# A linear-attention and feed-forward kernel on one core: one-pass softplus, exponentials gathered in two places of a tile, float32r earlier in the first tile

## The chip, the cores and the metric

The kernel runs on one core of one Trainium2 chip. A core has five engines that run side by side, each through its own queue in order: TensorE (PE, with weight loads counted apart as PEld) multiplies matrices, VectorE (DVE) and ScalarE (ACT) work element by element, GpSimd (POOL) does some of that too, and SyncE (SP) issues transfers. The metric is the device time of one execution in microseconds; lower is better. Results of matmuls land in PSUM, all other tiles lie in SBUF.

## What is computed

The inputs q, k, v have 8 batches, 8 heads, 576 positions and 64 columns. The attention has no matrix of scores; its output is laid out as 4608 tokens of 512 numbers and goes through two matrix products with a softplus between:

```python
q_s = softmax of q along the 64 columns
k_s = softmax of k along the 576 positions
kv = np.einsum('bhsd,bhse->bhde', k_s, v)
x = np.einsum('bhsd,bhde->bhse', q_s, kv)      # -> (4608, 512)
h = x @ w_in                                    # 512 -> 2048
g = np.maximum(h, 0.0) + np.log1p(np.exp(-np.abs(h)))
out = g @ w_out                                 # 2048 -> 512
```

## The kernel before

**Tiles and chunks.** The tokens are worked off in nine tiles of 512 (`SUBS`), the 2048 inner columns in sixteen chunks of 128 (`NJ`). For each tile t and chunk j, `up` (line 362) forms 128 x 512 numbers of h in a PSUM bank `ph` (there are two), `softplus` (line 377) turns them into g, and `down` (line 401) adds g times a chunk of `w_out` into four banks `po0` to `po3`, which `finish` (line 422) empties after the last chunk.

**Number formats.** In tiles 1 to 8 each operand of a product is split into a high part in float32r and a low part (the rest), and a product is three float32r matmuls: high x high, low x high, high x low (lines 372 to 374 and 416 to 418). `split_g` (line 393) makes g's parts, a copy on ScalarE and a subtraction on VectorE. In tile 0 both products are single float32 matmuls on unsplit operands (lines 367 and 412), which the profile records in two halves each.

**Weights.** They are 64-bit words holding one float each in an odd form, as the host only reinterprets them. `load_w` brings a chunk of both matrices in 1 MB; `top_w` and `scale_w` (ScalarE, lines 120 and 115), `sign_w` (VectorE, line 126; GpSimd for the first three chunks) and `join_w` (VectorE, line 136) make float32 in place. `split_w` (lines 140 to 146) makes the float32r parts, a cast on ScalarE and a subtraction on VectorE, in the buffer that the chunk before it has left.

**Softplus.** Four ScalarE passes (Abs, Exp, Copy, Ln; lines 384 to 387) and three VectorE passes (lines 388 to 390) form max(h, 0) + log1p(exp(-|h|)) over 128 x 512.

**Attention beside it.** While tile t goes through its chunks, `attend` lays out the attention of tile t+1 over the steps. `kv_unit` makes one pair of heads of a batch in six items: u0 maximum over positions held in a partition (VectorE), u1 and two TensorE transposes for the maximum across partitions (batches up to `ON_PE` = 2; GpSimd afterwards), u2 subtraction, u3 exponential on ScalarE and then 20 small matmuls on a PSUM bank `att`, u4 reciprocal of the sum, u5 scaling and splitting. Keys and values are loaded ahead, two buffers in turn, a new load following the matmuls. `q_unit` has twelve items, q0 to q11: maxima, exchange between partitions, subtraction, exponential, sums, reciprocal, product (for tile 1 the subtraction and product run on GpSimd, else on VectorE). `x_unit` makes x for one pair of heads in three items: x0 transposes q on VectorE into a bank, x1 splits it and multiplies with kv on TensorE, x2 splits the result. `x_first` and `split_whole` do this for tile 0 in float32.

**Order of the queues.** Everything runs under a schedule written out by hand: each engine's queue has the order in which the program emits. In step n (line 518) it emits `up` of slot n, attention's items, the weight work, `split_g` of slot n-1, the softplus of slot n, for tile 0 `top_w`, `scale_w`, `sign_w` of a later chunk, then `down` of slot n-2, and last the matmuls that attention's items have left in `waiting`.

In before, `join_w` runs for chunk j+1, the three passes ahead of it for chunk j+2, and `split_w` of the chunks goes on from step 10 to step 30, three in every four steps.

Of the kernel before, what the change touches and what calls it, by code (L numbers as in the profile page):

```python
# [8 lines left out]
F32 = mybir.dt.float32  # L9
F32R = mybir.dt.float32r  # L10
# [44 lines left out]
def tile_attn_ffn(  # L55
# [11 lines left out]
    const = ctx.enter_context(tc.tile_pool(name="const", bufs=1))  # L67
    xp = ctx.enter_context(tc.tile_pool(name="xp", bufs=1))
    gp = ctx.enter_context(tc.tile_pool(name="gp", bufs=2))
    tp = ctx.enter_context(tc.tile_pool(name="tp", bufs=1))  # L70
    wp = ctx.enter_context(tc.tile_pool(name="wp", bufs=1))
    qp = ctx.enter_context(tc.tile_pool(name="qp", bufs=1))
    kp = ctx.enter_context(tc.tile_pool(name="kp", bufs=2))
# [5 lines left out]
    nc.scalar.preload_act_table_set("natural_log_exp_and_others")  # L79
# [4 lines left out]
    zero = const.tile([P, 1], F32, name="zero")  # L84
    ident = const.tile([P, P], F32, name="ident")
    ln1 = const.tile([P, 1], F32, name="ln1")

# [52 lines left out]
    def split_w(k):  # L140

        y, _ = words(k, F32)
        parts[k] = wp.tile([P, 2, 2, DM], F32R, name=f"w{k - 1}" if k else "spare")
        hi, lo = (parts[k][:, i].rearrange("p z n -> p (z n)") for i in range(2))
        nc.scalar.copy(hi, y)
        nc.vector.tensor_tensor(out=lo, in0=y, in1=hi.bitcast(F32), op=ALU.subtract)  # L146
# [164 lines left out]
    def x_part(t, h):  # L311

        if h % 2 == 0 and (t, h // 2) not in xs:
            xs[t, h // 2] = xp.tile([P, 2, 2, TOK], F32R, name=f"x{(2 * t + h // 2 - 1) % 3}")
        return xs[t, h // 2][:, h % 2]

    def x_unit(t, h, ps):
# [41 lines left out]
        return [flip, product, take]  # L359


    def up(t, j):
        ph = ps_h.tile([P, TOK], F32, name="ph")
        if t == 0:
            y, _ = words(j, F32)
            for h in range(HP):
                nc.tensor.matmul(ph, lhsT=y[:, h * P:(h + 1) * P], rhs=x0[:, h], start=h == 0, stop=h == HP - 1)  # L367
            return ph
        for h in range(HP):
            w_hi, w_lo = (parts[j][:, i, 0, h * P:(h + 1) * P] for i in range(2))  # L370
            x_hi, x_lo = (x_part(t, h)[:, i] for i in range(2))
            nc.tensor.matmul(ph, lhsT=w_hi, rhs=x_hi, start=h == 0, stop=False)  # L372
            nc.tensor.matmul(ph, lhsT=w_lo, rhs=x_hi, start=False, stop=False)  # L373
            nc.tensor.matmul(ph, lhsT=w_hi, rhs=x_lo, start=False, stop=h == HP - 1)  # L374
        return ph

    def softplus(t, j, ph):

        if t == 0:
            u = tp.tile([P, TOK], F32, name=("u", "w", "l")[j % 3])  # L380
            w, l = (gp.tile([P, TOK], F32, name=name) for name in ("g_lo", "g_hi"))
        else:
            u, w, l = (tp.tile([P, TOK], F32, name=name) for name in ("u", "w", "l"))
        nc.scalar.activation(u, ph, AF.Abs)  # L384
        nc.scalar.activation(u, u, AF.Exp, scale=-1.0)  # L385
        nc.scalar.activation(w, u, AF.Copy, bias=1.0)  # L386
        nc.scalar.activation(l, u, AF.Ln, bias=1.0)  # L387
        nc.vector.scalar_tensor_tensor(out=w, in0=w, scalar=1.0, in1=u, op0=ALU.subtract, op1=ALU.subtract)  # L388
        nc.vector.scalar_tensor_tensor(out=w, in0=ph, scalar=0.0, in1=w, op0=ALU.max, op1=ALU.subtract)  # L389
        nc.vector.scalar_tensor_tensor(out=l, in0=l, scalar=ln1, in1=w, op0=ALU.subtract, op1=ALU.add)  # L390
# [10 lines left out]
    def down(t, j, g):  # L401
        if j == 0:
            acc[t] = [ps_o.tile([P, DM], F32, name=f"po{m}") for m in range(SUBS[t])]
        if t:
            g_hi, g_lo = g
            w_hi, w_lo = (parts[j][:, i, 1] for i in range(2))
        else:
            y, _ = words(j, F32)
        for m, po in enumerate(acc[t]):
            ms = slice(m * P, (m + 1) * P)  # L410
            if t == 0:
                nc.tensor.matmul(po, lhsT=g[:, ms], rhs=y[:, DM:2 * DM], start=j == 0, stop=j == NJ - 1)  # L412
                if j == NJ - 1:
                    finish(t, m)
                continue
            nc.tensor.matmul(po, lhsT=g_hi[:, ms], rhs=w_hi, start=j == 0, stop=False)  # L416
            nc.tensor.matmul(po, lhsT=g_hi[:, ms], rhs=w_lo, start=False, stop=False)  # L417
            nc.tensor.matmul(po, lhsT=g_lo[:, ms], rhs=w_hi, start=False, stop=j == NJ - 1)  # L418
            if j == NJ - 1:
                finish(t, m)  # L420

    def finish(t, m):

        if m == 0:
            outs[t] = (wp if t else xp).tile([P, SUBS[t], DM], F32, name=f"w{NJ - 1}" if t else "x0")
        o = outs[t][:, m]
        nc.scalar.activation(o, acc[t][m], AF.Copy, scale=1.0 / W_SCALE)
        a = START[t] + m * P
        nc.sync.dma_start(out=out[a:a + P, :], in_=o)
# [11 lines left out]
    with tc.manual_schedule():  # L441
# [8 lines left out]
        nc.vector.memset(zero, 0.0)  # L450

        nc.scalar.activation(ln1, zero, AF.Ln, bias=1.0)
# [31 lines left out]
        def attend(t):  # L484

            steps = [[] for _ in range(NJ + 1)]

            def lazy(make, slots):
                unit = []

                def step(i):
                    def fn():
                        if not i:
                            unit.extend(make())
                        unit[i]()
                    return fn

                for i, s in enumerate(slots):
                    steps[s].append(step(i))

            if t < B:
                on_pe = 1 if t <= ON_PE else 0
                for h in range(HP):
                    a = 2 * h
                    lazy(
                        lambda h=h: kv_unit(t, h, banks[h % 2], after=kv_prefetch),
                        [a, a + on_pe, a + 1 + on_pe, a + 2 + on_pe, a + 3 + on_pe, a + 3 + on_pe],
                    )
            lazy(lambda: q_unit(t), [3, 4, 5, 5, 6, 7, 8, 7, 8, 9, 9, 10])
            for h, slots in enumerate(([11, 11, 12], [12, 12, 13], [13, 13, NJ], [14, 14, NJ])):  # L510
                lazy(lambda h=h: x_unit(t, h, banks[h % 2]), slots)
# [76 lines left out]
```

## Time and profile before

| what | value |
|---|---|
| timed runs | 927.77 us median of 3 (927.75 to 928.3) |
| profiled execution | span 926.8 us, from the first to the last instruction; no other time of its own is recorded |
| PE, DVE, ACT, POOL busy | 887.3, 701.3, 582.6, 58.1 us |
| table loads on ScalarE | 1, of 1.283 us, at the start |
| softplus passes | ScalarE L384 to L387 0.60 to 0.63 us each; VectorE L388 to L390 0.69 to 0.83 us each |
| transfers | 45.09 MB read and 9.44 MB written from and to HBM, mostly in the first 60 us |

A line of the profile's groups gives the line of the kernel, the engine, the operation, output and input tiles by their names in the program, shapes, the count, then the busy time in total and the mean duration of one in nanoseconds, then how long the engine stood idle just before these instructions and what ended that. Rows of the timeline give the start and duration in microseconds. The end of a matmul is modelled, so matmuls overlap in the record: the distance from one start to the next is the true pace.

### The profile page before, as it was taken

The numbers are of one execution on the slowest core, as the hardware profiler recorded it, in microseconds if no ns is written. First come the engines' busy times: TensorE is split into PE (matmuls) and PEld (weight loads), VectorE is DVE, ScalarE is ACT, GpSimd is POOL, SyncE is SP. The second block draws the span as 40 slices with busy tenths as digits, with TensorE's granted clock in tenths as the row PEclk, the third lists the DMA queues.
The fourth block names the chain that finished last, engine by engine and source line by source line (L and its number), as shares of the span: only waits on it lengthen the run. The fifth ranks groups of instructions, "written<-read, shape, count | busy, mean of one in ns | idle before, by whom it ended". The sixth has DMA issues, their size and how long they took to land.

```text
span 926.8 us, 11611 instructions
## 1 busy us (share of the span) xinstructions
PE 887.3 (96%) x4196; PEld 676.1 (73%) x4196; DVE 701.3 (76%) x1094; ACT 582.6 (63%) x982; POOL 58.1 (6%) x119
## 2 busy tenths in 40 slices
PE   3789999989899999999999999999999999999998
PEld 2334444667688888888888888888888888888886
DVE  8777888788878877787788778877787757765553
ACT  4665676657666656666567566656665666566554
POOL 2202200000001100110011000100110000000000
PEclk9999999999999999999999999999999999999999
DMA  9970101111013101210121012101200110001001
GB/s 313 381 300 26 51 1 46 45 53 52 1 46 97 52 1 46 91 44 15 46 71 52 27 46 71 52 26 46 72 27 1 46 46 1 1 1 46 0 1 46
DMA packets 49034, 55.28 MB, mean 60 GB/s; under 512 B 2256, under 2 KB 39120, under 8 KB 47824
## 3 DMA queue, kind: packets, MB, share of 16 engines
q1 hardware_dynamic: 48400, 54.27, 17.5%
q8 instruction: 33, 0.54, 0.2%
q10 hardware_dynamic: 576, 0.26, 0.1%
q14 instruction: 25, 0.20, 0.1%
HBM read 45.09 MB, written 9.44 MB: 59 GB/s over the span
## 4 chain that ended last, share of the span: by engine, by line
PE 76%; DVE 11%; ACT 7%; DMA 4%; issue 3%; POOL 0%; SPq 0%; DVEq 0%; ACTq 0%; POOLq 0%
PE ph L372 11%; PE ph L374 11%; PE ph L373 11%; PE po L418 11%; PE po L417 11%; PE po L416 11%; PE po L412 3%; PE ph L367 3%; PE att L214 2%; DMA kvt<-in_kv 1%; DMA kvt<-in_kv_tail 1%; DVE l L390 1%; DVE w L389 1%; DVE w L388 1%; DVE w L126 1%
## 5 line engine op out<-in xcount | busy, mean ns | idle before, releaser
L372 PE MATMUL ph<-x,w 128*128 128x512 f32 x480 | 191.0, 398 | 0.0
L418 PE MATMUL po<-w,g_lo 128*128 128x512 f32 x480 | 187.1, 390 | 1.4 <-DVE g_lo L396 1.4
L374 PE MATMUL ph<-x,w 128*128 128x512 f32 x480 | 187.4, 390 | 0.0
L373 PE MATMUL ph<-x,w 128*128 128x512 f32 x480 | 187.1, 390 | 0.0
L417 PE MATMUL po<-w,g_hi 128*128 128x512 f32 x480 | 186.8, 389 | 0.0
L416 PE MATMUL po<-w,g_hi 128*128 128x512 f32 x480 | 186.7, 389 | 0.0
L388 DVE SCALAR_TENSOR_TENSOR w<-w,u 128x512 f32<-128x512 f32 x128 | 88.5, 691 | 109.6 <-ACT w L386 109.5
L395 ACT CAST g_hi<-l 128x512 fp32r<-128x512 f32 x128 | 79.7, 622 | 91.2 <-DVE l L390 90.6
L390 DVE SCALAR_TENSOR_TENSOR l<-l,ln,w 128x512 f32<-128x512 f32 x128 | 96.3, 752 | 15.0 <-DVE w L389 0.5
L418 PEld LDWEIGHTS po<-w,g_lo 128*128 128x128 f32 x480 | 90.1, 188 | 21.1 <-DVE g_lo L396 2.6
L372 PEld LDWEIGHTS ph<-x,w 128*128 128x128 f32 x480 | 90.4, 188 | 19.3 <-issue 0.6
L374 PEld LDWEIGHTS ph<-x,w 128*128 128x128 f32 x480 | 90.1, 188 | 19.4
L417 PEld LDWEIGHTS po<-w,g_hi 128*128 128x128 f32 x480 | 90.1, 188 | 18.7
L416 PEld LDWEIGHTS po<-w,g_hi 128*128 128x128 f32 x480 | 90.1, 188 | 18.7
L373 PEld LDWEIGHTS ph<-x,w 128*128 128x128 f32 x480 | 90.2, 188 | 17.5 <-DVE w L146 0.2
L396 DVE TENSOR_TENSOR g_lo<-l,g_hi 128x512 fp32r<-128x512 f32 x128 | 88.6, 692 | 15.6 <-ACT g_hi L395 15.3
L384 ACT ACTIVATE u<-ph 128x512 f32<-128x512 f32 x134 | 80.2, 599 | 31.4 <-PE ph L374 25.9
L387 ACT ACTIVATE l<-u 128x512 f32<-128x512 f32 x128 | 79.3, 619 | 26.7 <-DVE g_lo L396 26.1
L389 DVE SCALAR_TENSOR_TENSOR w<-ph,w 128x512 f32<-128x512 f32 x128 | 88.5, 691 | 4.4
L385 ACT ACTIVATE u<-u 128x512 f32<-128x512 f32 x134 | 84.7, 632 | 4.3
L386 ACT ACTIVATE w<-u 128x512 f32<-128x512 f32 x128 | 80.9, 632 | 4.1
L325 ACT CAST q_hi<-att 128x512 fp32r<-128x512 f32 x32 | 18.8, 587 | 78.9 <-DVE att L321 78.9
(127 smaller groups left out, 1064.1 us busy)
## 6 DMA issues: line engine op xcount, KB each, us to landing
kvt<-in_kv SPq DMA_DIRECT2D x30, 512.0 KB, 4.2
qt<-in_q SPq DMA_DIRECT2D x9, 1024.0 KB, 4.8
w<-in_w_in SPq DMA_DIRECT2D x16, 512.0 KB, 10.2
w<-in_w_out SPq DMA_DIRECT2D x16, 512.0 KB, 10.2
out<-w SPq DMA_DIRECT2D x32, 256.0 KB, 2.4
kvt<-in_kv_tail SPq DMA_DIRECT2D x28, 64.0 KB, 3.9
x<-in_kv SPq DMA_DIRECT2D x2, 512.0 KB, 9.3
out<-x SPq DMA_DIRECT2D x4, 256.0 KB, 2.4
```

Of the source, the lines that this page charges most:

```text
L372: nc.tensor.matmul(ph, lhsT=w_hi, rhs=x_hi, start=h == 0, stop=False)
L373: nc.tensor.matmul(ph, lhsT=w_lo, rhs=x_hi, start=False, stop=False)
L374: nc.tensor.matmul(ph, lhsT=w_hi, rhs=x_lo, start=False, stop=h == HP - 1)
L385: nc.scalar.activation(u, u, AF.Exp, scale=-1.0)
L386: nc.scalar.activation(w, u, AF.Copy, bias=1.0)
L388: nc.vector.scalar_tensor_tensor(out=w, in0=w, scalar=1.0, in1=u, op0=ALU.subtract, op1=ALU.subtract)
L389: nc.vector.scalar_tensor_tensor(out=w, in0=ph, scalar=0.0, in1=w, op0=ALU.max, op1=ALU.subtract)
L390: nc.vector.scalar_tensor_tensor(out=l, in0=l, scalar=ln1, in1=w, op0=ALU.subtract, op1=ALU.add)
L396: nc.vector.tensor_tensor(out=g_lo, in0=l, in1=g_hi.bitcast(F32), op=ALU.subtract)
L416: nc.tensor.matmul(po, lhsT=g_hi[:, ms], rhs=w_hi, start=j == 0, stop=False)
L417: nc.tensor.matmul(po, lhsT=g_hi[:, ms], rhs=w_lo, start=False, stop=False)
L418: nc.tensor.matmul(po, lhsT=g_lo[:, ms], rhs=w_hi, start=False, stop=j == NJ - 1)
```

## The change

- **Softplus** becomes one ScalarE activation, `AF.Softplus`, reading `ph` and writing a tile `l`; the three VectorE passes and the constants `zero` and `ln1` go. `tp` gets two buffers.
- **Table sets.** ScalarE's functions come in sets, of which one is loaded at a time. The set loaded first is now one with the exponential and without the logarithm. The softplus belongs to another set, so a load stands wherever an exponential follows a softplus or the other way round.
- **The plan.** The items of attention are placed by a table, `PLAN`: entry s lists what is emitted in step s of a tile (the 17th after the last chunk). All exponentials of a tile now stand in steps 3 and 8. Pairs of heads go together, u0 of heads 0 and 1 in one step, and so on, on both `att` banks.
- **float32r earlier.** Only chunks 0 to 3 of tile 0 (`EXACT` = 4) use single float32 matmuls; from chunk 4 on the products are split, as in the later tiles. For that x of tile 0 is split (`split_x0`, steps 0 and 1) and weights 4 to 15 are split two steps ahead of their use, in tile 0; weights 0 to 3 follow in steps 14 to 17. `top_w`, `scale_w`, `sign_w` run three chunks ahead instead of two, `join_w` two instead of one. All `split_whole` go to steps 0 and 1.
- **Buffers.** The split of weight 4 takes the spare buffer, the others again that of the chunk before; the x buffers turn by one place; all outputs leave through the buffer of weight 3.

```diff
+EXACT = 4
+PLAN = [
+    "u00 u10", "u01 u11", "u02 u12", "u03 u13 q0", "u04 u14 u05 u15 q1 q2", "u20 u30 q3", "u21 u31 q4", "u22 u32",
+    "u23 u33 q5 q6", "u24 u34 u25 u35 q7 q8 q9", "q10", "q11 x00 x01", "x02 x10 x11", "x12 x20 x21", "x30 x31", "",
+    "x22 x32",
+]
...
-    nc.scalar.preload_act_table_set("natural_log_exp_and_others")
+    nc.scalar.preload_act_table_set("exp_and_others")
...
-        parts[k] = wp.tile([P, 2, 2, DM], F32R, name=f"w{k - 1}" if k else "spare")
+        parts[k] = wp.tile([P, 2, 2, DM], F32R, name="spare" if k == EXACT else f"w{(k - 1) % NJ}")
...
+    def exact(t, j):
+        return t == 0 and j < EXACT
+
+    def split_x0(h):
+        x = x_part(0, h)
+        nc.scalar.copy(x[:, 0], x0[:, h])
+        nc.vector.tensor_tensor(out=x[:, 1], in0=x0[:, h], in1=x[:, 0].bitcast(F32), op=ALU.subtract)
...
-        nc.scalar.activation(u, ph, AF.Abs)
-        nc.scalar.activation(u, u, AF.Exp, scale=-1.0)
-        nc.scalar.activation(w, u, AF.Copy, bias=1.0)
-        nc.scalar.activation(l, u, AF.Ln, bias=1.0)
-        nc.vector.scalar_tensor_tensor(out=w, in0=w, scalar=1.0, in1=u, op0=ALU.subtract, op1=ALU.subtract)
-        nc.vector.scalar_tensor_tensor(out=w, in0=ph, scalar=0.0, in1=w, op0=ALU.max, op1=ALU.subtract)
-        nc.vector.scalar_tensor_tensor(out=l, in0=l, scalar=ln1, in1=w, op0=ALU.subtract, op1=ALU.add)
+    def softplus(ph):
+
+        l = tp.tile([P, TOK], F32, name="l")
+        nc.scalar.activation(l, ph, AF.Softplus)
         return l
...
-            outs[t] = (wp if t else xp).tile([P, SUBS[t], DM], F32, name=f"w{NJ - 1}" if t else "x0")
+            outs[t] = wp.tile([P, SUBS[t], DM], F32, name=f"w{EXACT - 1}")
...
-                if t == 0 and 1 <= j <= HP:
-                    split_whole(j - 1)
-                if t == 0 and 1 < j + 1 < NJ:
-                    join_w(j + 1)
-                for k in range(NJ):
-                    if n == 10 + 4 * k // 3:
-                        split_w(k)
+                if t == 0:
+                    if j < 2:
+                        split_whole(2 * j)
+                        split_whole(2 * j + 1)
+                    if j + 2 < NJ:
+                        join_w(j + 2)
+                        if j + 2 >= EXACT:
+                            split_w(j + 2)
+                    if j < 2:
+                        split_x0(2 * j)
+                        split_x0(2 * j + 1)
+                if 0 <= n - (NJ - 2) < EXACT:
+                    split_w(n - (NJ - 2))
...
             if soft:
-                pending.append((soft[0], split_g(soft[1]) if soft[0][0] else soft[1]))
+                pending.append((soft[0], soft[1] if exact(*soft[0]) else split_g(soft[1])))
                 soft = None
             if slot:
-                soft = slot, softplus(t, j, ph)
-                if t == 0 and 2 < j + 2 < NJ:
+                soft = slot, softplus(ph)
+                if t == 0 and j + 3 < NJ:
                     for fn in (top_w, scale_w, sign_w):
-                        fn(j + 2)
+                        fn(j + 3)
```

More of the change, by code (lines that the diff above doesn't have):

```diff
@@ L69, in tile_attn_ffn @@
     gp = ctx.enter_context(tc.tile_pool(name="gp", bufs=2))
-    tp = ctx.enter_context(tc.tile_pool(name="tp", bufs=1))
+    tp = ctx.enter_context(tc.tile_pool(name="tp", bufs=2))
     wp = ctx.enter_context(tc.tile_pool(name="wp", bufs=1))
@@ L83, in tile_attn_ffn @@
     banks = [ps_a.tile([P, 512], F32, name=f"att{i}") for i in range(2)]
-    zero = const.tile([P, 1], F32, name="zero")
     ident = const.tile([P, P], F32, name="ident")
-    ln1 = const.tile([P, 1], F32, name="ln1")
     raw, parts = {}, {}
@@ L313, in x_part @@
         if h % 2 == 0 and (t, h // 2) not in xs:
-            xs[t, h // 2] = xp.tile([P, 2, 2, TOK], F32R, name=f"x{(2 * t + h // 2 - 1) % 3}")
+            xs[t, h // 2] = xp.tile([P, 2, 2, TOK], F32R, name=f"x{(2 * t + h // 2 + 1) % 3}")
         return xs[t, h // 2][:, h % 2]
@@ L359, in x_first @@
         return [flip, product, take]
+    def exact(t, j):
[4 more added lines that the diff above has]
+        nc.vector.tensor_tensor(out=x[:, 1], in0=x0[:, h], in1=x[:, 0].bitcast(F32), op=ALU.subtract)
     def up(t, j):
         ph = ps_h.tile([P, TOK], F32, name="ph")
-        if t == 0:
+        if exact(t, j):
             y, _ = words(j, F32)
@@ L375, in up @@
         return ph
[L377 to L384, printed above, removed]
-        nc.scalar.activation(u, u, AF.Exp, scale=-1.0)
-        nc.scalar.activation(w, u, AF.Copy, bias=1.0)
-        nc.scalar.activation(l, u, AF.Ln, bias=1.0)
-        nc.vector.scalar_tensor_tensor(out=w, in0=w, scalar=1.0, in1=u, op0=ALU.subtract, op1=ALU.subtract)
-        nc.vector.scalar_tensor_tensor(out=w, in0=ph, scalar=0.0, in1=w, op0=ALU.max, op1=ALU.subtract)
-        nc.vector.scalar_tensor_tensor(out=l, in0=l, scalar=ln1, in1=w, op0=ALU.subtract, op1=ALU.add)
+    def softplus(ph):
+        l = tp.tile([P, TOK], F32, name="l")
+        nc.scalar.activation(l, ph, AF.Softplus)
         return l
@@ L403, in down @@
             acc[t] = [ps_o.tile([P, DM], F32, name=f"po{m}") for m in range(SUBS[t])]
-        if t:
+        if exact(t, j):
+            y, _ = words(j, F32)
+        else:
             g_hi, g_lo = g
             w_hi, w_lo = (parts[j][:, i, 1] for i in range(2))
-        else:
-            y, _ = words(j, F32)
         for m, po in enumerate(acc[t]):
             ms = slice(m * P, (m + 1) * P)
[L411 to L414, printed above, removed]
+            if exact(t, j):
+                nc.tensor.matmul(po, lhsT=g[:, ms], rhs=y[:, DM:2 * DM], start=j == 0, stop=False)
                 continue
@@ L449, in tile_attn_ffn @@
             load_w(k)
-        nc.vector.memset(zero, 0.0)
-        nc.scalar.activation(ln1, zero, AF.Ln, bias=1.0)
         whole = wp.tile([P, HP, P], F32, name="spare")
@@ L486, in attend, with lazy @@
             steps = [[] for _ in range(NJ + 1)]
-            def lazy(make, slots):
+            todo = {}
+            def lazy(prefix, n, make):
                 unit = []
@@ L492, in fn @@
                     def fn():
-                        if not i:
+                        if not unit:
                             unit.extend(make())
@@ L496, in step @@
                     return fn
-                for i, s in enumerate(slots):
-                    steps[s].append(step(i))
+                todo.update({f"{prefix}{i}": step(i) for i in range(n)})
             if t < B:
-                on_pe = 1 if t <= ON_PE else 0
                 for h in range(HP):
[L504 to L511, printed above, removed]
+                    lazy(f"u{h}", 6, lambda h=h: kv_unit(t, h, banks[h % 2], after=kv_prefetch))
+            lazy("q", 12, lambda: q_unit(t))
+            for h in range(HP):
+                lazy(f"x{h}", 3, lambda h=h: x_unit(t, h, banks[h % 2]))
+            for s, names in enumerate(PLAN):
+                steps[s] = [todo[name] for name in names.split() if name in todo]
             if t + 1 < NTILE:
```

## The prediction, made before the changed kernel ran

> **What bounds the kernel now.** First the head of the page, then busy time by stage, then single TensorE rows, to see where the stages begin.
>
> ```profile
> span 926.8 us, 11611 instructions
> ...
> PE 887.3 (96%) x4196; PEld 676.1 (73%) x4196; DVE 701.3 (76%) x1094; ACT 582.6 (63%) x982; POOL 58.1 (6%) x119
> ```
>
> ```profile
> 69.80:153.30 83.50, 81.45 (x248) 36.52 (x249) 69.16 (x95) 55.12 (x78) 10.64 (x13) 0.98 0.11 33
> 153.30:255.00 101.70, 93.68 (x449) 69.00 (x448) 82.33 (x126) 65.97 (x108) 1.95 (x12) 1.00 0.11 36
> 255.00:349.50 94.50, 94.49 (x488) 77.19 (x487) 75.78 (x120) 60.93 (x108) 6.36 (x16) 1.00 0.15 48
> ```
>
> The windows give the length, then busy us (and count) of PE, PEld, DVE, ACT and POOL, the granted clock and DMA. The third stretch, one steady tile, leaves PE 0.01 us idle: there nothing but fewer matmuls can help, and VectorE and ScalarE are off the path. The second, most of tile 1, leaves PE 8.0 us idle. The page's 96% hides this difference.
>
> ```profile
> 34.23 0.59 PE L367 MATMUL ph<-x,w 128*128 128x512 f32 x1
> ...
> 159.70 0.82 PE L372 MATMUL ph<-x,spare 128*128 128x512 f32 x1
> ...
> 267.25 0.39 PE L372 MATMUL ph<-x,spare 128*128 128x512 f32 x1
> ...
> 269.97 0.39 PE L416 MATMUL po<-w,g_hi 128*128 128x512 f32 x1
> ...
> 361.72 0.39 PE L372 MATMUL ph<-x,spare 128*128 128x512 f32 x1
> ```
>
> These are the first matmuls of tiles 0, 1 and 2, the first `down` matmul after chunk 0 of tile 2, and the first of tile 3. Tile 0 takes 159.70-34.23 = 125.5 us from first `up` to first `up`, tile 1 107.5, tile 2 94.5. Everything from tile 2 on is paced by matmuls that the change doesn't touch. The forecast is therefore: when does tile 1 start, and how long does it take?
>
> **The matmuls of tile 0.** The chain of waits has float32 `up` and `down` of one chunk:
>
> ```profile
> 153.25 3.43 PE ph L367 x8
> 156.68 3.60 PE po L412 x8
> ```
>
> A float32 chunk is 7.0 us. In float32r 12 matmuls take 269.97-267.25 = 2.72 us, a chunk 5.44. Twelve chunks save 12 x 1.6 = 19 us of TensorE, if TensorE sets the pace there.
>
> **The new ring in tile 0.** The added work is on the other two engines. Rows of what a chunk of tile 0 will need (line engine op, operands, count | busy, mean ns | idle before):
>
> ```profile
> L384 ACT ACTIVATE u<-ph 128x512 f32<-128x512 f32 x134 | 80.2, 599 | 31.4 <-PE ph L374 25.9 <-PE ph L367 3.8 <-issue 1.2
> L120 ACT ACTIVATE w<-w 128x1024 uint32<-128x1024 uint8 x16 | 18.3, 1142 | 1.0 <-DMA w<-in_w_out 1.0
> L115 ACT ACTIVATE w<-w 128x1024 f32<-128x1024 f32 x16 | 18.2, 1140 | 0.0
> L126 DVE TENSOR_SCALAR w<-w 128x1024 uint8<-128x1024 uint8 x13 | 17.5, 1349 | 6.3 <-ACT w L115 6.1
> L136 DVE SCALAR_TENSOR_TENSOR w<-w 128x1024 uint32<-128x1024 uint32 x16 | 19.4, 1213 | 0.0
> L145 ACT CAST w<-w 128x1024 fp32r<-128x1024 f32 x15 | 16.8, 1120 | 0.1
> L146 DVE TENSOR_TENSOR w<-w,w 128x1024 fp32r<-128x1024 f32 x15 | 18.3, 1220 | 1.0 <-ACT w L145 1.0
> L395 ACT CAST g_hi<-l 128x512 fp32r<-128x512 f32 x128 | 79.7, 622 | 91.2 <-DVE l L390 90.6
> L396 DVE TENSOR_TENSOR g_lo<-l,g_hi 128x512 fp32r<-128x512 f32 x128 | 88.6, 692 | 15.6 <-ACT g_hi L395 15.3
> ```
>
> Both engines take their queue in order. In step n ScalarE's queue will hold: attention's items, cast of weight n+2 (L145), cast of g(n-1) (L395), softplus(n), `top_w` and `scale_w` of weight n+3. VectorE's: attention's items, `join_w`(n+2), the low half (L146), g's low half, `sign_w`(n+3). So softplus(n) stands behind cast(n+2), which waits for join(n+2), which waits for sign(n+2), which waits for scale(n+2), which stands behind softplus(n-1): a ring, one turn a step. Waiting behind the cast are g's cast and softplus, hence `down`; behind sign and join all of attention on VectorE. Before, the cast starts only at step 10, at 0.75 a step, and TensorE's 7.0 us covered it; that cover is gone.
>
> The softplus itself has no row. ScalarE's passes over 128x512 lie between 0.587 (L325 below) and 0.622; I take 0.60, that of L384, which also reads PSUM. A turn: 0.60 + 1.14 + 1.14 + 1.35 + 1.21 + 1.12 + 0.62 = 7.18, less some 0.1 where ScalarE passes follow each other (four times), plus three hand-overs of some 0.05: 7.0 us. That is above 5.44. What three VectorE and three ScalarE passes less per chunk free doesn't shorten it: they weren't in it.
>
> On top comes attention's work where it stands between sign and join, or between casts:
>
> ```profile
> L182 DVE TENSOR_REDUCE mx<-kvt 128x128 f32<-128x640 f32 x30 | 39.8, 1326 | 3.7 <-DMA kvt<-in_kv_tail 3.7
> L203 DVE TENSOR_TENSOR kvt<-kvt,att 128x640 f32<-128x640 f32 x8 | 6.6, 826 | 0.2
> L278 DVE TENSOR_REDUCE m<-qt 128x32 f32<-128x1024 f32 x18 | 21.7, 1210 | 0.3 <-DMA qt<-in_q 0.3
> L265 DVE COPY other<-m 32x64 f32<-32x64 f32 x32 | 6.0, 186 | 0.6
> L209 ACT ACTIVATE kvt<-kvt 128x640 f32<-128x640 f32 x30 | 22.1, 741 | 0.0
> L293 ACT ACTIVATE qt<-qt 128x1024 f32<-128x1024 f32 x18 | 19.0, 1056 | 3.4 <-DVE qt L290 1.7 <-POOL qt L290 1.5
> L321 DVE STREAM_TRANSPOSE att<-qt 128x512 f32<-128x512 f32 x32 | 23.2, 724 | 0.0
> L325 ACT CAST q_hi<-att 128x512 fp32r<-128x512 f32 x32 | 18.8, 587 | 78.9 <-DVE att L321 78.9
> L326 DVE TENSOR_TENSOR q_lo<-att,q_hi 128x512 fp32r<-128x512 f32 x32 | 22.1, 692 | 21.3 <-ACT q_hi L325 21.3
> L340 DVE TENSOR_TENSOR x<-att,x 128x512 fp32r<-128x512 f32 x32 | 21.3, 686 | 0.0
> L79 ACT ACT_TABLE_LOAD x1 | 1.3, 1283 | 0.7 <-PEq L577 0.7
> ```
>
> By the plan, in us: step 4 (u4, u5 of two heads, q1, q2: 1.21 + 13 small pieces at 0.19 + 0.6 for a ScalarE piece between) 4.3; step 5 (two maxima) 2.65; step 6 0.5; step 7 1.65; step 8 3.3; step 9 (2 x 1.21 + 14 small + 0.6) 5.7; step 10 0; step 11 (flip, cast, low half) 2.0; steps 12 and 13 2.7 each, one L340 more. Sum 25.5. Step 8: table load 1.28, exponentials 2 x 0.74 + 2 x 1.06, less overlaps 4.5, against 2.5 for sign and join beside them: 2.0 too long; then a load back to softplus, 1.28.
>
> **The sum to tile 1.** Up to step 3 chunks are exact, and TensorE sets the pace: from 34.2, `up` 3.4; 1.2 for the second head's maximum, since two transposes stand before the next `up`; `up` 3.4; some 1.5 until VectorE, with a join and a sign ahead, reaches the second reductions; `up` and `down` 7.0: softplus(2), behind `down` and a cast, at about 51.5. The turn of step 3 holds q0 (1.21) and the load back, but no cast of g: 7.0 - 0.6 + 1.2 + 1.3 = 8.9 (its first load and two exponentials hide beside sign, q0 and join): 60.4. Ten turns, the first without g: 70 - 0.5 + 25.5 = 95.0: softplus(13) at 155.4. Then g's cast and low half come through, and TensorE does `down`(12), an attention product, `up`(15), `down`(13): 1.5 + 3 x 2.72 + 0.9 = 10.6. Tile 1 starts at 166.0.
>
> GpSimd's four q passes run beside the ring, and one VectorE row shows what such an overlap can do:
>
> ```profile
> 110.30 2.40 DVE L388 SCALAR_TENSOR_TENSOR g_lo<-g_lo,u 128x512 f32<-128x512 f32 x1
> ```
>
> 2.40 where the neighbours need 0.69. Between 0 and 4 x 1.7 us; I take 1.5, about one such hit, as near to this row as to none. So 167.5: **tile 0 becomes 7.8 us longer**, though its matmuls became shorter.
>
> **What tile 1 gives back.** Two weight splits remain in it instead of sixteen, and three VectorE passes a chunk are gone, so its PE idle goes; next in line is TensorE, at tile 2's 94.5. With 0.5 for the eight transposes of its attention, which tile 2 hasn't got, 95.0 instead of 107.5. Tile 2 starts at 262.5 instead of 267.25: 4.8 us gained.
>
> **The rest.** Table loads in later tiles: step 8 gives ScalarE 1.3 + 1.5 + 2.1 + 0.6 + 1.3 + 0.6 = 7.4 us between two softplus ends, while the `up` that needs the freed bank starts over 10 us on: nothing. K-v pairs: a tile's matmuls are 16 x 5.44 = 87.0 of 94.5, so eight attention products with their gaps cost 7.5; pairing saves at least nothing and at most half the k-v part, some 2 a tile. I take 0.2 over six tiles, 1.2, nearer nothing, because PE is busy throughout. The pairs' keys load two at a time, needed two steps after the bank is read: over 10 us, covered. The end of the kernel stays.
>
> 926.8 - 4.8 - 1.2 = 920.8 of span. The timed median is 927.77, 1.0 above this span; forecast **921.7**. A 0.2% difference is about what a measurement can tell from none: 925.9 to 929.6 is "same".
>
> **Rivals.** *A, forecast*: 0.57, 912 to 930 by itself (an error of 0.5 us a turn is 7 us over 14 turns).
>
> *B, a table switch costs double*, 2.57, because the queue must run empty around it. In tile 0 three switches and a part of a fourth (step 3's first) lie on the ring, 3.5 x 1.28: 4.5 us more, 926.2. For it: no row shows a load between two passes; against: the one row says 1.28. 0.20. The Trainium skill, "ScalarE: Activation LUTs", section "What ACT_TABLE_LOAD costs", gives 1283 ns for the load, as the row here, plus some 1380 ns of drain for every switch; by its 2.66 the result would be an estimated 926.5.
>
> *C, slower: the clock falls in tile 0.* TensorE now idles about 3 us a step there. At half clock a step is 2 x 5.44 + 0.9 = 11.8, above a mean turn of 9.5: ten steps x 2.3 = 23 us, 945. It costs something below a granted clock of 0.67 through tile 0 (6.34/9.5) and makes the kernel slower below 0.62. For it: the 0.98 of tile 0's window above; against: that is small, and matmuls still fill two thirds of each step. 0.11. The Trainium skill, "TensorE: Matmul & The Clock Gate", Part 1, halves the clock after an idle window of about 3.4 us; the gaps here are just under that.
>
> *D, no ring*: casts and softplus interleave and TensorE paces tile 0. `up`s and `down`s 4 x 3.4 + 12 x 2.72 + 4 x 3.6 + 10 x 2.72 = 88 and attention 8: tile 1 starts at 130, 37 us earlier than forecast, 885. For it: busy sums alone; against: the order of the queues. 0.08.
>
> *E, the change doesn't do what it says*: the set with softplus lacks the copies, and every chunk switches twice: 14 x 2.57 = 36 us, 957. One load serves copies too in the trace of before, so unlikely: 0.04.
>
> Faster: most of A (0.48), D, and nearly half of B: 0.64; same 0.15; slower, the tail of A, a little of B, C and E: 0.21. The range drops D, E and most of C: 909 to 931.
>
> **What would show it.** Tile 1's first float32r `up` near 167 (before 159.7), tile 2's near 262; in tile 0 casts L145 idle until join, softplus late after its `up`; PE's busy share in tile 0 near two thirds; no PE idle in tile 1; 94 a tile after. Tile 1 starting by 150 would refute the ring; later than 172 with a granted clock near 1, the price of a turn.

## The result, and the profile after

The changed kernel takes **913.14 us** (median of 4 runs, 911.88 to 915.36) against 927.77 before (four runs, too): a ratio of **0.984, 95% interval 0.9823 to 0.9857**, 14.6 us less. The forecast was 921.7, a gain of 6.1. The time lies in the range of 909 to 931 and the direction was right, but the gain was more than twice as large. The profiled execution spans 911.7 us against 926.8, 15.1 less.

The head of the page of the changed kernel:

```profile
span 911.7 us, 10863 instructions
...
PE 867.4 (95%) x4292; PEld 701.0 (77%) x4292; DVE 413.3 (45%) x677; ACT 378.7 (42%) x596; POOL 50.5 (6%) x119
```

VectorE went from 76% to 45% and ScalarE from 63% to 42%, and the span shrank by 1.6%: the busy shares alone don't tell what a change is worth. The first matmul of tiles 0, 1, 2 and 3 in the changed kernel's timeline of TensorE:

```profile
33.62 0.59 PE L381 MATMUL ph<-x,w 128*128 128x512 f32 x1
...
163.19 0.39 PE L386 MATMUL ph<-x,w 128*128 128x512 f32 x1
...
257.78 0.39 PE L386 MATMUL ph<-x,w 128*128 128x512 f32 x1
...
351.10 0.39 PE L386 MATMUL ph<-x,w 128*128 128x512 f32 x1
```

Differences of such rows, for all tiles, give the account of the gain (us; "to `up` of tile t+1" is the length of tile t):

| stretch | before | after | difference |
|---|---|---|---|
| to the first `up` | 34.23 | 33.62 | -0.6 |
| tile 0 | 125.47 | 129.57 | +4.1 |
| tile 1 | 107.55 | 94.59 | -13.0 |
| tiles 2 to 6, each | 94.47 to 94.81 | 93.08 to 94.09 | -5.4 in all |
| tile 7, tile 8 and the end | 186.4 | 186.2 | -0.2 |

The windows of the changed kernel (length, busy us and count of PE, PEld, DVE, ACT, POOL, granted clock, DMA):

```profile
33.60:163.20 129.60, 107.17 (x442) 73.06 (x441) 91.67 (x118) 80.34 (x105) 15.62 (x17) 0.91 0.32 116
69.80:153.30 83.50, 62.69 (x268) 47.26 (x266) 56.29 (x66) 48.04 (x62) 10.02 (x10) 0.86 0.05 15
153.30:255.00 101.70, 101.70 (x530) 84.37 (x529) 50.30 (x85) 44.80 (x73) 1.89 (x12) 1.00 0.17 55
255.00:349.50 94.50, 94.50 (x494) 78.48 (x494) 42.87 (x74) 38.74 (x64) 4.72 (x16) 1.00 0.15 48
```

In tile 0 no engine is full: in the second row PE has 62.69 of 83.5 us, VectorE 56.29, ScalarE 48.04. That fits a ring, in which each engine waits for another in turn. The clock of 0.86 is a mean; the last section has what it is made of. From tile 1 on PE has no idle time left in these rows.

One turn of the ring, step 6 of tile 0. First ScalarE's timeline of the changed kernel (start, duration), from one softplus (L394) to the next:

```profile
79.48 0.59 ACT L394 ACTIVATE l<-ph 128x512 f32<-128x512 f32 x1
79.97 1.16 ACT L126 ACTIVATE w<-w 128x1024 uint32<-128x1024 uint8 x1
81.00 1.13 ACT L121 ACTIVATE w<-w 128x1024 f32<-128x1024 f32 x1
85.23 1.12 ACT L151 CAST w<-w 128x1024 fp32r<-128x1024 f32 x1 [3.10 <-DVE w L142]
86.26 0.62 ACT L399 CAST g_hi<-l 128x512 fp32r<-128x512 f32 x1
86.78 0.59 ACT L394 ACTIVATE l<-ph 128x512 f32<-128x512 f32 x1
```

and VectorE's in the gap:

```profile
82.16 1.33 DVE L132 TENSOR_SCALAR w<-w 128x1024 uint8<-128x1024 uint8 x1 [1.24 <-ACT w L121]
83.52 0.49 DVE L204 TENSOR_REDUCE m<-att 128x1 f32<-128x128 f32 x2
83.93 1.22 DVE L142 SCALAR_TENSOR_TENSOR w<-w 128x1024 uint32<-128x1024 uint32 x1
```

Softplus, `top_w` (L126), `scale_w` (L121), then `sign_w` (L132) and `join_w` (L142) on VectorE while ScalarE idles 3.10 us in front of the split's cast (L151); then the cast, g's cast (L399), the next softplus: 86.78 - 79.48 = 7.30 us, one behind the other. 0.5 of it is attention's reduction L204 between sign and join.

### The profile page after: what moved, and what is told of

It is laid out like the page before. It is cut to its first block, busy times and chain, and to the rows that moved or that the text cites. A ratio compares the mean times of both kernels' runs of the same rounds, so it can differ in the third digit from the quotient of the medians.

```text
span 911.7 us, 10863 instructions
## 1 busy us (share of the span) xinstructions
PE 867.4 (95%) x4292; PEld 701.0 (77%) x4292; DVE 413.3 (45%) x677; ACT 378.7 (42%) x596; POOL 50.5 (6%) x119
## 4 chain that ended last, share of the span: by engine, by line
PE 84%; DVE 7%; ACT 5%; issue 2%; DMA 1%; POOL 0%; ACTq 0%; DVEq 0%; POOLq 0%
PE ph L386 13%; PE po L420 13%; PE po L418 13%; PE po L419 13%; PE ph L388 13%; PE ph L387 13%; PE att L220 2%; DVE w L132 2%; DVE w L142 2%; ACT w L126 1%; ACT w L121 1%; PE att L338 1%; PE att L339 1%; PE att L337 1%; DMA qt<-in_q 1%
## 5 line engine op out<-in xcount | busy, mean ns | idle before, releaser
L418 PE MATMUL po<-w,g_hi 128*128 128x512 f32 x524 | 205.9, 393 | 9.2 <-ACT g_hi L399 9.2
L420 PE MATMUL po<-w,g_lo 128*128 128x512 f32 x524 | 205.9, 393 | 3.4 <-DVE g_lo L400 3.4
L386 PE MATMUL ph<-x,w 128*128 128x512 f32 x524 | 208.0, 397 | 0.0
L419 PE MATMUL po<-w,g_hi 128*128 128x512 f32 x524 | 205.5, 392 | 0.0
L387 PE MATMUL ph<-x,w 128*128 128x512 f32 x524 | 205.2, 392 | 0.0
L388 PE MATMUL ph<-x,w 128*128 128x512 f32 x524 | 205.1, 391 | 0.0
L400 DVE TENSOR_TENSOR g_lo<-l,g_hi 128x512 fp32r<-128x512 f32 x140 | 97.5, 697 | 231.1 <-ACT g_hi L399 231.1
L394 ACT ACTIVATE l<-ph 128x512 f32<-128x512 f32 x144 | 86.2, 599 | 193.9 <-PE ph L388 193.7
L399 ACT CAST g_hi<-l 128x512 fp32r<-128x512 f32 x140 | 86.8, 620 | 120.3 <-PE po L419 117.8
L418 PEld LDWEIGHTS po<-w,g_hi 128*128 128x128 f32 x524 | 99.2, 189 | 30.6 <-ACT g_hi L399 10.3
L419 PEld LDWEIGHTS po<-w,g_hi 128*128 128x128 f32 x524 | 99.4, 190 | 20.9
L388 PEld LDWEIGHTS ph<-x,w 128*128 128x128 f32 x524 | 99.0, 189 | 21.3
L386 PEld LDWEIGHTS ph<-x,w 128*128 128x128 f32 x524 | 99.5, 190 | 20.3 <-issue 0.3
L387 PEld LDWEIGHTS ph<-x,w 128*128 128x128 f32 x524 | 99.2, 189 | 19.9 <-issue 0.3
L346 DVE TENSOR_TENSOR x<-att,x 128x512 fp32r<-128x512 f32 x32 | 21.4, 691 | 105.7 <-ACT x L345 105.7
L345 ACT CAST x<-att 128x512 fp32r<-128x512 f32 x32 | 18.0, 589 | 69.1 <-PE att L339 38.7
L188 DVE TENSOR_REDUCE mx<-kvt 128x128 f32<-128x640 f32 x30 | 39.3, 1318 | 11.0 <-POOL mx L193 7.6
L332 DVE TENSOR_TENSOR q_lo<-att,q_hi 128x512 fp32r<-128x512 f32 x32 | 22.1, 692 | 32.8 <-ACT q_hi L331 32.8
L193 POOL PARTITION_ALL_REDUCE mx<-mx x20 | 14.1, 705 | 297.6 <-DVE mx L188 230.5
```

The source lines that it names most:

```text
L188: nc.vector.tensor_reduce(out=mx, in_=kt.rearrange("p c z d -> p z d c"), op=ALU.max, axis=AX.X)
L332: nc.vector.tensor_tensor(out=q_lo, in0=ps, in1=q_hi.bitcast(F32), op=ALU.subtract)
L346: nc.vector.tensor_tensor(out=x[:, 1], in0=ps, in1=x[:, 0].bitcast(F32), op=ALU.subtract)
L394: nc.scalar.activation(l, ph, AF.Softplus)
L399: nc.scalar.copy(g_hi, l)
L400: nc.vector.tensor_tensor(out=g_lo, in0=l, in1=g_hi.bitcast(F32), op=ALU.subtract)
```

## The experiments

Each kernel was timed beside the kernel before on the same chip, and the ratio is to that run of it, with a 95% interval. The tile lengths, in us from first `up` to first `up`, are of one profiled execution each; the first `up` of tile 0 itself starts anywhere from 32.0 to 35.4 us.

| kernel | median us | ratio | tile 0 | tile 1 | tiles 2 to 6, mean |
|---|---|---|---|---|---|
| before | 927.77 | 1 | 125.5 | 107.55 | 94.63 |
| the change | 913.14 | 0.984 [0.9823, 0.9857] | 129.6 | 94.59 | 93.55 |
| softplus alone | 921.99 | 0.993 [0.9915, 0.9946] | 129.3 | 99.23 | 94.38 |
| plan alone | 943.95 | 1.0174 [1.0142, 1.0206] | 125.2 | 104.65 | 98.26 |
| softplus and plan | 913.17 | 0.984 [0.9819, 0.9862] | 126.5 | 96.86 | 93.55 |
| split one step ahead | 898.31 | 0.9669 [0.9655, 0.9684] | 114.3 | 94.59 | 93.55 |
| cast doubled | 926.93 | 0.9984 [0.9974, 0.9995] | 143.8 | 94.59 | 93.55 |
| `up` doubled in tile 0 | 920.17 | 0.9911 [0.9882, 0.994] | 137.8 | 94.59 | 93.55 |
| k-v products apart | 921.41 | 0.9922 [0.9904, 0.9939] | 129.7 | 95.95 | 94.93 |
| softplus and plan, 3 buffers | 902.16 | 0.9716 [0.9695, 0.9736] | 115.9 | 96.86 | 93.55 |
| the change, 3 buffers | 913.67 | 0.9841 [0.9812, 0.9869] | 129.6 | 94.59 | 93.55 |
| split one step ahead, 3 buffers | 895.11 | 0.964 [0.9624, 0.9656] | 109.9 | 94.59 | 93.55 |

**Is the ring what sets tile 0?** Three edits of the changed kernel touch it. The first emits each tile-0 split a step later, when its join has long run, and ahead of the next join:

```diff
+                    if EXACT <= j + 1 < NJ:
+                        split_w(j + 1)
                     if j + 2 < NJ:
                         join_w(j + 2)
-                        if j + 2 >= EXACT:
-                            split_w(j + 2)
```

> The changed kernel, with a weight's split emitted one step ahead of its use and before the next weight's join, instead of two steps ahead and behind it. Same instructions, another order. Ring theory: the cast no longer waits for a sign and join of its own step, so softplus isn't held up; ScalarE and VectorE need some 6.5 us a step, near TensorE's 6.3. Tile 1 starts at 142 to 146 us instead of 163.2, the later tiles keep their lengths: 891 to 896 us. Rival, tile 0 is slow because TensorE's clock is low there or because of VectorE's total work: tile 1 starts at 158 or later, 908 or more.

Measured 898.31, tile 1 starting at 146.66: 16.5 us earlier than in the changed kernel, with the same instructions in another order. It fell a little short of what was expected, 142 to 146 for tile 1 and 891 to 896 for the time. ScalarE's casts in tile 0 (count | busy, mean | idle before, releaser), first the changed kernel:

```profile
L151 ACT CAST w<-w 128x1024 fp32r<-128x1024 f32 x14 | 15.7, 1119 | 32.7 <-DVE w L142 32.4 <-DVE w L152 0.3
```

then with the split one step ahead:

```profile
L151 ACT CAST w<-w 128x1024 fp32r<-128x1024 f32 x14 | 15.7, 1123 | 9.3 <-DVE w L142 7.6 <-DVE w L152 1.6
```

Same casts, same 1.12 us, but 7.6 us of waiting for the join in place of 32.4. The order of the queue, not the amount of work, held tile 0.

The second edit issues the cast of chunks 4 to 15 twice, which adds work and leaves the order:

```diff
-        nc.scalar.copy(hi, y)
+        for _ in range(2 if k >= EXACT else 1):
+            nc.scalar.copy(hi, y)
```

> The changed kernel with ScalarE's cast of a split weight chunk (1.12 us each, chunks 4 to 15) issued twice, whichever tile it stands in. Ring theory: the cast is one link of tile 0's ring, so each of its turns gets about 1.1 us longer; tile 0 from 129.6 to 139-143, time 923-928. Rival, tile 0 is set by TensorE's matmuls (ScalarE is busy for less than half of it): tile 0 within 3 us of 129.6, time 913-917.

Tile 0 grew by 143.8 - 129.6 = 14.2 us for 12 extra casts, a little above the 139 to 143 expected, and the time by 13.8 to 926.93: some 1.15 to 1.19 for each, about the cast's full length. All other tiles kept their lengths to 0.01 us, although ScalarE was busy for 80.34 of tile 0's 129.6 us. The third adds TensorE work, the float32r `up` matmuls of tile 0 twice:

```diff
-        for h in range(HP):
...
+        for _ in range(2 if t == 0 else 1):
+            for h in range(HP):
...
```

> The changed kernel with the twelve float32r `up` matmuls of each split chunk of tile 0 (chunks 4 to 15) issued twice, which adds twelve times 2.72, 32.6 us of matmul. Ring theory: TensorE is not in the ring's turn (12 turns of 7.0 us plus extras, about 9 us a step; a step's matmuls become 8.2), so most of it goes into TensorE's idle time: tile 0 from 129.6 to 130-142, time 914-926, and its granted clock in tile 0 no lower. Rival, TensorE's matmuls pace tile 0: tile 0 near 162, time near 946.

Of 32.6 us of added matmul, tile 0 shows 137.8 - 129.6 = 8.2, and none of that is in the ring. The turns of steps 4 to 13, from one softplus to the next, are the changed kernel's to within 0.06 us, the shortest too (7.28 against 7.30 in step 6, 7.54 against 7.54 in step 10), though a step now has 5.44 + 2.72 = 8.16 us of matmuls. The 8 us come behind the ring, where TensorE works off what is left: from softplus(13) to tile 1's first `up` it takes 169.77 - 151.43 = 18.3 us in place of 10.3. The two rows in the timelines of ScalarE and TensorE:

```profile
151.43 0.59 ACT L395 ACTIVATE l<-ph 128x512 f32<-128x512 f32 x1
...
169.77 0.39 PE L387 MATMUL ph<-x,w 128*128 128x512 f32 x1
```

The window from 58 to 163 us, of the changed kernel:

```profile
58.00:163.00 105.00, 84.19 (x372) 62.81 (x367) 71.54 (x93) 61.02 (x80) 13.11 (x16) 0.89 0.16 48
```

and of the one with `up` doubled:

```profile
58.00:163.00 105.00, 101.27 (x460) 80.16 (x459) 67.99 (x88) 56.26 (x74) 12.18 (x10) 0.97 0.16 47
```

PE's busy time rises by 17, the granted clock from 0.89 to 0.97, and the ring's turns stay as they were.

**Which part of the change pays?** The softplus in one pass, put into the kernel before with nothing else ("Softplus" and "Table sets" of the change):

```diff
-        nc.scalar.activation(u, ph, AF.Abs)
...
+        l = tp.tile([P, TOK], F32, name="l")
+        nc.scalar.activation(l, ph, AF.Softplus)
```

> The kernel before with the one-pass softplus alone; exponentials stay in five places of a tile, so ten table loads a tile instead of four. If VectorE's relief is what shortens tile 1 and loads are hidden by TensorE: tile 1 near 97.5 instead of 107.5, tiles 2 to 6 some 0.25 us shorter each, 912 to 915 us. If the loads count (1.3 us each, six more a tile): 920 or more.

921.99, as expected if the loads count (920 or more), and with a smaller gain than the 912 to 915 of the other case. Tile 1 fell by 8.3 us and the steady tiles by 0.25 each, but tile 0 grew by 3.8. ScalarE's waits in tile 0 of this kernel (waiting instruction, what for: us, times, longest):

```profile
ACT L378 <- PE po L400: 22.0, 4, 10.3
ACT l L378 <- PE po L400: 14.5, 8, 4.4
```

L378 is the softplus; the first row is the table load in front of it; L400 is the exact `down`. In tile 0 `down` reads softplus' result itself, and there are two buffers, so softplus(n) waits for `down` of chunk n-2, with `top_w` and `scale_w` of a later weight behind it. In before the same wait stood ahead of the last of the four passes alone, when the first three had been done, and was short:

```profile
ACT g_hi L387 <- PE po L412: 9.8, 7, 1.7
```

9.8 us in seven waits, against 36.5 in twelve. A pass that does the whole work in one piece starts the whole of it after the wait. Eleven table loads, 14.1 us of ScalarE, stand in tile 0 beside this; how the 3.8 us divide between the two was not separated. (With the plan added below, tile 0 has five loads, still 44 us of such waits, and is 126.5 us long.)

The plan alone, in the kernel before with its seven-pass softplus:

```diff
-            lazy(lambda: q_unit(t), [3, 4, 5, 5, 6, 7, 8, 7, 8, 9, 9, 10])
+            lazy("q", 12, lambda: q_unit(t))
...
+            for s, names in enumerate(PLAN):
+                steps[s] = [todo[name] for name in names.split() if name in todo]
```

> The kernel before with the plan alone: softplus in seven passes, float32 in tile 0. If pairing the k-v products is what shortens tiles 2 to 6: 0.85 us a tile less, 94.6 to 93.8, tile 1 about 2 us less, 920 to 923 us. If the shorter tiles come from VectorE's relief: tiles 2 to 6 stay at 94.6, 925 to 928.

Both expectations failed: it is *slower*, by 1.4% to 2.1%, the steady tiles by 3.6 us each. In tile 3 step 11 takes 435.20 - 426.59 = 8.61 us where it is 6.15 in before. VectorE's timeline of this kernel leading up to it:

```profile
418.31 1.24 DVE L247 SCALAR_TENSOR_TENSOR kv_lo<-att,r,kv_hi 64x64 fp32r<-64x64 f32 x4 [0.50 <-ACT kv_hi L244]
419.56 2.35 DVE L302 TENSOR_REDUCE s<-qt 128x32 f32<-128x1024 f32 x2
...
426.23 1.22 DVE L310 TENSOR_TENSOR qt<-qt,s 128x1024 f32<-128x1024 f32 x1
...
432.21 0.72 DVE L327 STREAM_TRANSPOSE att<-qt 128x512 f32<-128x512 f32 x1
```

Step 9 of the plan brings all of this together. With three softplus passes a step on top, VectorE seems to fall behind: the transpose of q at 432.21 comes so late that TensorE waits for what it leads to (q's low half, L332; us, times, longest):

```profile
PE att L337 <- DVE q_lo L332: 2.1, 1, 2.1
```

With the one-pass softplus in place the same plan gains, as the next run shows, so the plan needs the room that it makes. Both together, without float32r in tile 0 (the two edits above in one):

> The kernel before with the one-pass softplus and the plan, but tile 0 wholly in float32 and weights split in steps 10 to 30 as before: the change without its float32r part. Ring theory: no ring, since casts begin at step 10 and stand behind joins of the step before; tile 0 as before or 2 to 3 us shorter (tile 1 starts at 156 to 158), tile 1 about 96.5, tiles 2 to 6 about 93.3: 907 to 911 us, less than the changed kernel's 913. Rival, the float32r matmuls bring what they save on TensorE: 918 or more.

913.17, ratio 0.984: the same as the whole change, just above the 907 to 911 expected and not less than the changed kernel. Against softplus alone the plan is worth 0.83 us in each steady tile. **The third part, float32r in tile 0, nets nothing**: tile 0 is 3.1 us longer with it (129.57 against 126.46), tile 1 2.3 shorter (94.59 against 96.86). The largest gain of the change, tile 1's 13.0 us, is divided by these runs as well, in the order in which the parts were added: 8.3 come with the softplus (107.55 to 99.23), 2.4 with the plan (to 96.86), 2.3 with float32r.

**What are the k-v pairs worth?** In the changed kernel, the products of heads 1 and 3 go to a list that is emptied after the next `up`:

```diff
-            later(products)
+            (later if not b or h % 2 == 0 else held.append)(products)
...
                 ph = up(t, j)
+                for products in held:
+                    products()
+                held.clear()
```

> The changed kernel with the k-v products of heads 1 and 3 emitted after the next `up` again, so that no two stand side by side on TensorE. If pairing halves nothing but the products' own time (a single one was 0.98 us, a pair 1.54), each of tiles 2 to 6 gets 0.84 us longer, 93.1-94.1 becomes 93.9-94.9, tiles 0 and 1 at most 0.8 each: time 917-920. Rival, the forecast's own term of 0.2 us a tile: pitches as they were, time 913-915.

921.41, above the expected 917 to 920; each of tiles 2 to 6 got 1.38 us longer. The steps of tile 2 tell why. Steps 3 and 4, and again 8 and 9, are together 12.83 us where the changed kernel has 12.42: 0.41 twice, 0.82, the price expected. The other 0.55 is in step 10, 5.99 in place of 5.44, a wait that the edit made. PE's timeline of this kernel:

```profile
321.28 0.50 PE L421 MATMUL po<-w,g_lo 128*128 128x512 f32 x1 [0.24 <-DVE g_lo L401]
```

In VectorE's queue the scaling of kv, which the later product makes late, stands ahead of g's low half. So the pairing itself is worth 0.82 a tile.

**Is the wait for `down` real, and does the ring swallow it?** Three buffers for softplus' result, `tile_pool(name="tp", bufs=3)` for `bufs=2`, in three kernels:

> The kernel before with the one-pass softplus and the hand-written plan (no float32r in tile 0), and with three buffers for softplus' result instead of two. Theory: in tile 0 softplus(n) waits for the exact `down` of n-2 that reads the buffer; with a third buffer that wait goes, and tile 0 falls from 126.5 to 110-118, time 897-905. Rival, the chain of sign, join and the next `up` sets tile 0's turn whether softplus is early or not: tile 0 within 3 us of 126.5, time 910-914.

> The changed kernel with three buffers for softplus' result and nothing else. The wait of softplus(n) for `down` of n-2 stands only in the first chunks of tile 0, where `down` reads the result itself; the ring behind chunk 4 stays. Theory: tile 0 from 129.6 to 124-128, time 907-912. Rival, the ring takes it up (softplus early, cast late all the same): 129.6 and 912-914.

> The changed kernel with each tile-0 split emitted one step ahead (898.3 in its own run, tile 0 114.3), and three buffers for softplus' result. In this version l is read by `split_g` within a step, except in the four exact chunks: the theory gives only the exact chunks' waits back, tile 0 110-114, time 894-898. Rival, no wait on l is left in the ring: within 0.2% of 898.3.

Softplus and plan: tile 0 fell from 126.5 to 115.9, as the theory had it, and of the 44 us in which softplus waited for `down` none is left. Tile 0 of this kernel is then TensorE's:

```profile
33.50:149.40 115.90, 113.30 (x353) 52.36 (x351) 78.01 (x96) 63.44 (x81) 16.43 (x17) 1.00 0.36 130
```

PE 113.30 of 115.90 us busy at a clock of 1.00. In the changed kernel the third buffer did nothing (129.60 against 129.57), against the theory and as its rival had it. With two buffers, too, no softplus in tile 0 of the changed kernel is recorded as waiting for `down`, so there was nothing to give back. With the split one step ahead there was one such wait, of 3.5 us, and with the third buffer it is gone. Tile 0 became 4.4 us shorter (109.9 against 114.3), but its first `up` came 3.0 later (35.38 against 32.39), so tile 1 starts only 1.4 earlier; the median fell by 3.2. That version, **895.11 us, ratio 0.964 [0.9624, 0.9656]**, is the fastest of all and beats both kernels. Its tile 0:

```profile
35.40:145.30 109.90, 101.04 (x442) 69.62 (x441) 93.36 (x117) 80.22 (x105) 15.71 (x17) 0.97 0.36 131
```

With the split moved, float32r does show its shorter matmuls: tile 0 is 114.3 against 126.5 with two buffers, 109.9 against 115.9 with three. PE is still idle for 8.9 of these 109.9 us; in 6.5 of them `up` waits for the parts of a split weight (L151 and L152).

## Why the prediction was right in direction and wrong in size

**The new ring in tile 0: right, to 0.6 us in each turn.** Its turns against the sums that the prediction gives (bare turn 7.0, plus the step's extras; starts of softplus in ScalarE's timeline 59.10, 69.94, 79.48, 86.78, 94.92, 104.97, 118.02, 125.56, 134.29, 143.59, 152.91):

| step | 4 | 5 | 6 | 7 | 8 | 9 | 10 | 11 | 12 | 13 |
|---|---|---|---|---|---|---|---|---|---|---|
| forecast | 10.8 | 9.65 | 7.5 | 8.65 | 10.3 | 12.7 | 7.0 | 9.0 | 9.7 | 9.7 |
| measured | 10.84 | 9.54 | 7.30 | 8.14 | 10.05 | 13.05 | 7.54 | 8.73 | 9.30 | 9.32 |

The sum is 93.8 where 95.0 was forecast. Moving the split (tile 0 down by 15.3), doubling the cast (up by 14.2) and doubling `up` (turns unchanged) show that it sets the time. TensorE's matmuls became 12 x 1.6 = 19 us shorter without shortening tile 0, as forecast.

**The sum to tile 1: 4.3 us too late** (163.19 against 167.5), from five small terms: softplus(2) 1.0 too late (50.46 against 51.5), the turn of step 3 0.3 too long, the ten turns 1.2, the end 0.3 (163.19 - 152.91 = 10.3 against 10.6), and 1.5 for the collision with GpSimd, which the ten turns as measured already hold. It occurs in two places. VectorE's timeline of the changed kernel, in step 5 and in step 10:

```profile
72.62 1.87 DVE L132 TENSOR_SCALAR w<-w 128x1024 uint8<-128x1024 uint8 x1 [1.06 <-ACT w L121]
...
119.04 2.40 DVE L400 TENSOR_TENSOR g_lo<-l,g_hi 128x512 fp32r<-128x512 f32 x1
121.36 1.30 DVE L132 TENSOR_SCALAR w<-w 128x1024 uint8<-128x1024 uint8 x1
```

and GpSimd's beside them:

```profile
67.65 5.68 POOL L296 TENSOR_TENSOR qt<-qt,m 128x1024 f32<-128x1024 f32 x2 [8.20 <-DVE m L293]
...
115.34 5.55 POOL L310 TENSOR_TENSOR qt<-qt,s 128x1024 f32<-128x1024 f32 x2 [12.67 <-DVE s L307]
```

In step 10 the low half takes 2.40 us beside GpSimd's product, as in the row that the prediction had of before. That low half isn't in the ring; it only pushes the sign behind it, and step 10 is 0.5 us longer than bare. In step 5 it is the sign itself, a link of the ring, that overlaps GpSimd's subtraction and takes 1.87 us where its others take 1.30 to 1.34. So some 1.0 of the 1.5 came true, if the overlap is the cause in both places. The good fit of step 5 (9.54 against 9.65) is then in part luck, and the ten turns without collisions were priced some 2.2 too high, not 1.2.

**What tile 1 gives back: right.** 94.59 against 95.0, with no PE idle in the rows shown. Tile 2 starts at 257.8, 4.7 before the forecast's 262.5: that is the 4.3 of tile 0 and 0.4 here.

**"The rest": the step that failed.** The span shrank by 9.1 us more than forecast (15.1 against 6.0). 4.7 of them lie ahead of tile 2 and are sizes, the terms just listed; the other 4.4 lie behind it, where a reason was wrong. "Everything from tile 2 on is paced by matmuls that the change doesn't touch" leaves out that the change regroups them. The prediction put k-v pairs at "0.2 over six tiles, 1.2, nearer nothing, because PE is busy throughout". Tiles 2 to 6 alone gave 5.4. The reasoning was the wrong way round: where PE is the bound and busy throughout, whatever it is spared counts in full; nothing hides it. And the price stood in before's timeline. One product apart, between two ordinary steps of tile 2:

```profile
278.13 0.39 PE L372 MATMUL ph<-x,w 128*128 128x512 f32 x1
...
283.66 0.80 PE L214 MATMUL att<-kvt 128*64 128x65 f32 x20
284.39 0.50 PE L372 MATMUL ph<-x,w 128*128 128x512 f32 x1
...
289.99 0.39 PE L372 MATMUL ph<-x,w 128*128 128x512 f32 x1
```

and a pair in the changed kernel:

```profile
274.10 0.39 PE L386 MATMUL ph<-x,w 128*128 128x512 f32 x1
...
279.63 1.39 PE L220 MATMUL att<-kvt 128*64 128x65 f32 x40
280.95 0.50 PE L386 MATMUL ph<-x,spare 128*128 128x512 f32 x1
...
286.52 0.39 PE L386 MATMUL ph<-x,w 128*128 128x512 f32 x1
```

Two steps with one product are 289.99 - 278.13 = 11.86 us, with a pair 286.52 - 274.10 = 12.42, without any 2 x 5.44 = 10.88. A single product is worth 0.98, a pair 1.54, so two pairs for four singles save 2 x (1.96 - 1.54) = 0.84 a tile, 4.2 in five tiles. The separated version gave 0.82 back. The other 1.2 us or so of the 5.4 comes with the softplus: alone, it took 0.25 off each steady tile. The kernel before has single late steps (step 13 of tile 3: 444.78 - 437.92 = 6.86 us) where the one with softplus alone has none (438.49 - 432.31 = 6.18).

**Table loads in later tiles: nothing, right.** The kernel with softplus alone has 75 loads behind the first one, the changed kernel 31, and their steady tiles differ by 0.83 us, which pairing accounts for. What the plan pays here is pairs, not saved loads.

**Rivals.** *B, a table switch costs double*: refuted by ScalarE's timeline of the changed kernel, where steps 2 and 3 meet and in step 8:

```profile
52.01 1.11 ACT L121 ACTIVATE w<-w 128x1024 f32<-128x1024 f32 x1
53.13 1.28 ACT L215 ACT_TABLE_LOAD   x1
54.43 1.38 ACT L215 ACTIVATE kvt<-kvt 128x640 f32<-128x640 f32 x2
...
103.04 0.62 ACT L399 CAST g_hi<-l 128x512 fp32r<-128x512 f32 x1
103.68 1.28 ACT L394 ACT_TABLE_LOAD   x1
104.97 0.60 ACT L394 ACTIVATE l<-ph 128x512 f32<-128x512 f32 x1
```

The load starts as the pass before it ends (53.13 after 52.01 + 1.11), and the next pass starts 1.30 us later. From g's cast to softplus it is 104.97 - 103.04 = 1.93 us with a load between, and 86.78 - 86.26 = 0.52 without, in the turn shown above: some 1.4 us in all, the load and the overlap of two passes that it takes away. The Trainium skill, "ScalarE: Activation LUTs", section "What ACT_TABLE_LOAD costs", adds a drain of about 1380 ns to each switch; its 1283 ns for the load is in this trace, the drain is not. *C, the clock falls in tile 0*: it did, to a mean of 0.86 in the window above, and TensorE's gaps weren't all near 3 us: in step 9 it stood idle for 7.7 us. It cost the ring nothing that the profile shows. These are the waits of ScalarE that the profile lists for the changed kernel from 59.1 to 153 us (as above: us, times, longest), and none is for TensorE's matmuls:

```profile
ACT w L151 <- DVE w L142: 31.5, 9, 5.8
ACT q_hi L331 <- DVE att L327: 6.2, 3, 2.1
ACT kv_hi L244 <- DVE r L230: 3.3, 2, 1.7
```

*D, no ring*, with tile 1 starting at 130: even with the ring loosened and the third buffer it starts at 145.28. *E, copies outside the softplus' set*: no load stands between a softplus and a cast in the turn shown.

## What to carry to other kernels

Where an engine is shown busy throughout, price each of its instructions that a change spares in full, by the distance between starts of ordinary steps with and without them; where none is busy throughout, look for a ring through in-order queues, and try moving one emission by a step before making any work shorter. A pass that does all its work in one piece needs its buffer free when it starts: look who still reads the one that it will overwrite. Parts of a change can need each other: here the plan without the cheaper softplus lost 1.7%, and with it gained 1.0% (921.99 to 913.17).

## What the runs showed of the hardware

- **The granted clock was full or half, never between, and cost nothing where TensorE was not the bound.** In the changed kernel's tile 0 it is half in four stretches, 76.2 to 79.6, 96.7 to 100.1, 113.7 to 127.4 and 141.0 to 144.4 us, and full in the rest; the mean is 0.91. One stretch before such a drop, and the longest at half clock:

```profile
93.20:96.60 3.40, 1.29 (x5) 0.49 (x4) 1.92 (x3) 3.22 (x5) 0.00 (x0) 1.00 0.00 0
113.70:127.40 13.70, 7.13 (x16) 5.15 (x17) 10.67 (x13) 7.69 (x10) 5.55 (x2) 0.50 0.00 0
```

  In the 3.4 us ahead of each of the four, PE was busy for 0.33, 1.29, 0.04 and 1.14 us; ahead of the second no single gap was over 1.6. At half clock a float32r matmul starts every 0.43 us in place of 0.23. So a fuller TensorE kept more of the full clock: in tile 0 PE was busy for 98% of the stretch at a mean of 1.00 (softplus and plan with three buffers), 92% at 0.97 (the fastest version), 83% at 0.91 (the changed kernel). These busy shares hold matmuls that the half clock drew out.
- **A table load cost itself and one overlap.** 1.283 us, and some 1.4 from pass to pass on ScalarE, as shown above; and 44 more of them (75 against 31) made the steady tiles no longer beyond what pairing explains, as ScalarE has room there.
- **A group of small matmuls cost more than its matmuls**: 20 of them added 0.98 us, 40 of them 1.54, so by these two sizes some 0.42 (2 x 0.98 - 1.54) goes with each group.
- **The one-pass softplus reading PSUM was as long as the passes that it replaced**: 0.599 us on average for 128x512 (144 of them), as the Abs of before, which also reads PSUM.
